# Weighted values as plain float32 products on TensorE, in place of float16 parts and DMA transposes

## The chip, the cores and the metric

The kernel runs on one core of one Trainium2 chip. The metric is the device time of one execution in microseconds (us); the time before is the median of three runs. Engines are named as in the profile: PE is the matrix engine, PEld its weight loads, DVE, ACT and POOL the vector, scalar and GpSimd engines, SP the queue that issues the DMAs.

## The reference

Attention over 2 batches of 8 heads, 576 positions and head size 64, and then two feed-forward blocks over the 1152 rows of 512 features:

```
q_rot, k_rot = rotate(q), rotate(k)                   # rotary embedding
scores = (q_rot @ k_rot.T) / 8
attn = exp(scores - max(scores)); attn /= sum(attn) + 1e-9
x = attn @ v                                          # heads side by side: 1152 x 512
x = ((x @ w_a) * (x @ w_b)) @ w_out                   # 512 -> 1536 -> 512
h = x @ w_in                                          # 512 -> 2048
out = (h * tanh(softplus(h))) @ w_out2                # 2048 -> 512
```

## The kernel before, in words

**Units.** The eight heads of a batch are handled as four pairs (p = 0 to 3 for batch 0, 4 to 7 for batch 1). A pair has nine units n: for each head four blocks of 128 query rows, and one unit "rest" that holds the last 64 rows of both heads. That makes 72 units, 36 in each batch. Each unit makes its scores on PE (tile `s`, two halves of 288 columns, a high and a low part of k each, so four matmuls), takes the row maximum (`m`, DVE), the exponential E (ACT), brings E to the layout with keys on the partitions, and multiplies it by V into tile `o` (`weighted`). V has a column of ones ahead of its 64 columns, so that column 0 of `o` is the sum. `finish` (L748) divides by it, and `transpose_x` turns the result into the columns of `x` that the feed-forward block reads.

**E transposed and multiplied.** Both operands are held as two float16 parts, high and low, and three partial products are added up. V is scaled by a power of two per pair (`v_max`, `v_scale`, `v_split`, L609 to L648; tile `vhl`) so that its parts fit float16. In batch 0 (`attend0`, L692) PE transposes E in float32 into PSUM (`tm`: four 128-column chunks of a unit; `tr`: the last chunk of two units together), ACT casts that to the high part and DVE subtracts for the low part (`ptm`, `ptr`); a unit has 15 float16 products. In batch 1 (`attend`, L725) ACT and DVE split E first (`pp`), and a DMA transpose on SP's queue writes the transposed parts (`pt`); a unit has 14 products there, the low parts against a second copy of V (`vh2`, L586) that `v_split` makes by DMA.

**Feed-forward.** Layer 1 and layer 2 of the first block (tile `l`, 1728 matmuls of 256 or 320 columns over both batches) and the second block (tiles `h` and `acc`) use float32 operands held as two reduced-precision parts in three passes. Each weight tile is unpacked by three DVE instructions (`xw`), cast by ACT and subtracted by DVE or POOL (`w`).

**Order.** The program is recorded as a list of operations with due times (`at(t)`) and costs (`Plan.cost`, L260), and `Plan.order` (L284) makes one fixed order per engine out of it: an operation is taken by due time among those that are ready by the planner's own clock. Operations marked `any` go to DVE or POOL and those marked `flex` to ACT or DVE, by the planner's costs. On the chip each engine works through its list strictly in that order. Layer 1 of batch 0 is put between the attention units of batch 1, since it needs only batch 0.

**PSUM.** `s` has two buffers of two banks, `o` one bank (a second one, `o2_ps`, in batch 1); in batch 0 `tm` has two and `tr` one, in batch 1 `l` has two.

Of the kernel before, what the change touches and what calls it, by code (L numbers as in the profile page):

```python
# [20 lines left out]
NP = H // 2  # L21
# [149 lines left out]
class Plan:  # L171
# [30 lines left out]
    def record(self, engine, method, args, kw):  # L202
# [26 lines left out]
        if key == "flex":  # L229

            scale = kw["scale"]
            forms = (
                ("act", "activation", args + (AF.Copy,), dict(scale=scale)),
                ("dve", "tensor_scalar_mul", args + (scale,), {}),
            )
            method, args, kw = forms[0][1:]
# [23 lines left out]
    def cost(self, key, method, out, args, kw, views):  # L260
# [146 lines left out]
VM = 4  # L407
# [10 lines left out]
VP = (10, 5, 8)  # L418
# [31 lines left out]
def kernel(ctx: ExitStack, tc: tile.TileContext, qk, v5, w1, w2, w34, tab, out):  # L450
# [34 lines left out]
    t_cm, t_ps = open_pool("t_ps", 1, space=PSUM)  # L485
    o2_ps = None
# [52 lines left out]
    ones = a_p.tile([8, 128], F32, tag="ones", name="ones")  # L539
# [7 lines left out]
    vhl = [(a_p if i < 2 else a0_p).tile([128, 5, 2, 130], F16, tag=f"vhl{i}", name=f"vhl{i}") for i in range(3)]  # L547

    vh2 = [a_p.tile([128, 4, 2, 66], F16, tag=f"vh2{i}", name=f"vh2{i}") for i in range(2)]

    vr = [a0_p.tile([128, 2, 130], F16, tag=f"vr{i}", name=f"vr{i}") for i in range(3)]
    vb = (0, 1, 2, 0, 1, 0, 1, 0)
# [18 lines left out]
    def load_v(p, pool_, tag, bufs):  # L571
        b, c = divmod(p, NP)
        t = pool_.tile([128, 512 if tag == "raw" else 5 * D], I64, tag=tag, name=f"v{p}", bufs=bufs)
        t = t.bitcast(F32)[:, 0 : 10 * D]
        sp.dma_start(t, v5[b, c].rearrange("p c h d -> p (c h d)"))
        return t
# [26 lines left out]

    v_mx = a_p.tile([128, B * NP], F32, tag="v_mx", name="v_mx")
    v_up = a_p.tile([128, B * NP], F32, tag="v_up", name="v_up")

    def v_max(p):  # L609
        if p < VM:  # L610

            of = vhl[min(p, len(vhl) - 1)].rearrange("p c h e -> p (c h) e")[:, :, 1 : D + 1]
            act.activation(of, v_t[p].rearrange("p (n d) -> p n d", d=D), AF.Abs, accum_out=v_mx[:, p : p + 1])
            return
        dve.tensor_reduce(v_mx[:, p : p + 1], v_t[p], axis=AX.X, op=ALU.max, apply_absolute_value=True)

    def v_scale(p0, p1):
        n, t = p1 - p0, o_ps.tile([128, 512], F32, tag="o", name=f"vs{p0}")
        m = a_p.tile([n, 1 + n], F32, tag=f"vm{p0}", name=f"vm{p0}")
        mx, up = v_mx[:, p0:p1], v_up[:, p0:p1]  # L620
        pe.matmul(t[0:n, 0:128], lhsT=mx, rhs=ident[:, 0:128], start=True, stop=True)
        dve.tensor_reduce(m[:, 0:1], t[0:n, 0:128], axis=AX.X, op=ALU.max)
        dve.tensor_scalar_mul(m[:, 1 : 1 + n], ident[0:n, 0:n], m[:, 0:1])
        pe.matmul(t[:, 128 : 128 + n], lhsT=ones[0:n, :], rhs=m[:, 1 : 1 + n], start=True, stop=True)
        dve.tensor_scalar(mx, t[:, 128 : 128 + n], 1e-30, 1e30, op0=ALU.max, op1=ALU.min)
        dve.tensor_scalar(mx.bitcast(U32), mx.bitcast(U32), 0x7F800000, None, op0=ALU.bitwise_and)
        dve.tensor_scalar_mul(mx, mx, 2.0**-14)
        dve.reciprocal(up, mx)

    def v_split(p):  # L630
        of = vhl[vb[p]].rearrange("p c h e -> p (c h) e")
        vt, up = v_t[p].rearrange("p (n d) -> p n d", d=D), v_up[:, p : p + 1]
        hi = of[:, :, 1 : D + 1]
        act.activation(hi, vt, AF.Copy, scale=up)
# [522 lines left out]
```

## Time and profile before

| what | value |
|---|---|
| time, median of 3 runs | 629.03 us (627.71 to 632.53) |
| time of the profiled execution | 626.95 us |
| its span, first to last instruction | 624.8 us |
| PE busy | 575.8 us (92%), 4384 matmuls |
| DVE busy | 493.1 us (79%) |
| ACT busy | 319.0 us (51%) |
| POOL busy | 127.4 us (20%) |
| granted clock, mean | 0.98 of full speed |

The span has four stretches, by what PE does: attention of batch 0 up to about 113 us; attention of batch 1 with layers 1 and 2 of batch 0 between its units, 113 to 295 us; the rest of the first block, 295 to 420 us; the second block from there. A busy PE is not a PE at its peak: a matmul's duration holds its way through the array, and the next one starts long before it ends. What PE can do is read from the distance of the starts in a dense stretch.

### The profile page before, as it was taken

Reading aid. Unit: us, or ns where it says so; the run is one execution under the profiler, and the core shown is the slowest. Engines: PE = TensorE matmul, PEld = TensorE weight load, DVE = VectorE, ACT = ScalarE, POOL = GpSimd, SP = SyncE. Lnnn points to the kernel's source line nnn. Section 1 sums busy time; section 2 is a strip of 40 time slices with the busy share of each in tenths; the row PEclk is TensorE's granted clock in tenths of the full one; section 3 lists DMA queues with packets and bytes.
Section 4 is the critical chain, followed back from the end, with each engine's and each line's share of the span. In section 5 each row is a group of like instructions: output and inputs, shape, how many; then the busy total and the mean of one; then the engine's idle time right before and its main releaser. Section 6 shows DMA issues by size and latency. Waiting matters only on the chain.

```text
span 624.8 us, 11406 instructions
## 1 busy us (share of the span) xinstructions
PE 575.8 (92%) x4384; PEld 526.8 (84%) x4384; DVE 493.1 (79%) x956; ACT 319.0 (51%) x629; POOL 127.4 (20%) x124
## 2 busy tenths in 40 slices
PE   6687888988898897999999999999999999999997
PEld 5576777987787786999999999997888899988985
DVE  6889989999899999999999999979999334332221
ACT  4978888674664754453344443246444444442320
POOL 5567683555315400120000001000000000000000
PEclk8898999999899898999999999999999999999999
DMA  8024212767569575879965557767897224220002
GB/s 300 6 72 163 87 41 69 213 144 204 144 155 250 136 176 123 203 184 242 375 210 201 171 202 231 292 203 252 277 301 264 67 69 152 77 75 1 0 1 84
DMA packets 78917, 100.27 MB, mean 160 GB/s; under 512 B 50832, under 2 KB 52496, under 8 KB 78864
## 3 DMA queue, kind: packets, MB, share of 16 engines
q1 hardware_dynamic: 78864, 99.55, 53.6%
q8 instruction: 34, 0.56, 0.4%
q14 instruction: 19, 0.16, 0.1%
HBM read 77.50 MB, written 10.75 MB: 141 GB/s over the span
## 4 chain that ended last, share of the span: by engine, by line
PE 65%; DVE 18%; ACT 8%; DMA 4%; POOL 3%; issue 2%; SPq 0%; POOLq 0%; DVEq 0%; ACTq 0%
PE l L389 28%; PE acc L389 16%; PE h L389 15%; DVE xw L389 5%; DVE m L389 3%; PE s L389 2%; PE o L389 2%; DMA pt<-pp 2%; ACT e L389 2%; POOL qkr L389 2%; DVE qk L389 2%; ACT qk L389 1%; DVE pp L389 1%; DVE w L389 1%; ACT ptm L389 1%
## 5 line engine op out<-in xcount | busy, mean ns | idle before, releaser
L389 PE MATMUL l<-x,w 128*128 128x256 f32 (+1 forms) x1152 | 169.2, 302 | 6.3 <-ACT w L389 2.3
L389 PEld LDWEIGHTS l<-x,w 128*128 128x128 f32 x1152 | 158.4, 192 | 8.6 <-DVE ab L389 2.8
L389 DVE SCALAR_TENSOR_TENSOR xw<-wr,xw 128x512 uint32<-128x512 uint32 x208 | 147.3, 722 | 1.0
L389 PE MATMUL h<-y,w 128*128 128x320 f32 (+1 forms) x576 | 105.0, 336 | 0.9 <-DVE g L389 0.9
L389 PE MATMUL acc<-w,g 128*128 128x512 f32 x432 | 105.6, 396 | 0.0
L389 PEld LDWEIGHTS h<-y,w 128*128 128x128 f32 x576 | 93.5, 188 | 10.4 <-DVE g L389 1.3
L389 ACT CAST w<-xw 128x512 fp32r<-128x512 f32 x97 | 59.8, 622 | 70.7 <-DVE xw L389 60.0
L389 PEld LDWEIGHTS acc<-w,g 128*128 128x128 f32 x432 | 80.6, 188 | 18.1
L389 PE MATMUL l<-ab,w 128*128 128x320 f32 (+1 forms) x576 | 80.2, 297 | 0.0
L389 PEld LDWEIGHTS l<-ab,w 128*128 128x128 f32 x576 | 77.2, 190 | 0.1
L389 DVE TENSOR_TENSOR w<-wc,w 128x512 fp32r<-128x512 f32 x39 | 26.7, 691 | 53.6 <-ACT w L389 52.3
L389 DVE TENSOR_TENSOR w<-xw,w 128x512 fp32r<-128x512 f32 x81 | 58.1, 722 | 5.6 <-ACT w L389 5.3
L389 PE MATMUL s<-qk 128*128 128x288 f32 x128 | 42.4, 345 | 14.6 <-ACT e L389 5.7
L389 DVE TENSOR_REDUCE m<-s 128x1 f32<-128x576 f32 x72 | 53.5, 748 | 2.7 <-PE s L389 2.4
L389 DVE TENSOR_SCALAR xw<-wr 128x512 uint32<-128x512 uint32 x104 | 51.7, 509 | 4.6 <-DMA wr<-in_w_dram 4.3
L389 ACT ACTIVATE h<-h 128x320 f32<-128x320 f32 (+1 forms) x48 | 22.8, 475 | 57.4 <-PE h L389 57.3
L389 DVE TENSOR_TENSOR g<-h,g 128x320 fp32r<-128x320 f32 (+1 forms) x48 | 26.6, 555 | 28.4 <-ACT g L389 28.3
L389 POOL TENSOR_TENSOR qkr<-qkr,cs 128x576 f32<-128x576 f32 x28 | 43.8, 1581 | 22.4 <-DMA qkr<-in_qk_dram 22.2
L389 PEld LDWEIGHTS s<-qk 128*128 128x128 f32 x128 | 25.8, 202 | 20.3 <-ACT e L389 9.0
L389 ACT ACTIVATE s<-s,m 128x576 f32<-128x576 f32 x36 | 25.7, 717 | 32.2 <-DVE m L389 31.7
L389 ACT CAST w<-wc 128x512 fp32r<-128x512 f32 x39 | 23.9, 617 | 35.6 <-PE acc L389 33.7
L389 POOL TENSOR_TENSOR w<-xw,w 128x512 fp32r<-128x512 f32 x16 | 20.5, 1280 | 96.8 <-ACT w L389 96.8
(93 smaller groups left out, 760.6 us busy)
## 6 DMA issues: line engine op xcount, KB each, us to landing
wr<-in_w_dram SPq DMA_DIRECT2D x104, 512.0 KB, 4.2
wc<-kc SPq DMA_DIRECT2D x39, 256.0 KB, 2.9
kc<-xw SPq DMA_DIRECT2D x32, 256.0 KB, 2.6
qkr<-in_qk_dram SPq DMA_DIRECT2D x14, 576.0 KB, 4.8
v<-in_v_dram SPq DMA_DIRECT2D x8, 320.0 KB, 6.4
out_dram<-o_sb SPq DMA_DIRECT2D x9, 256.0 KB, 2.1
pt<-pp SPq DMA_TRANSPOSE x36, 3.7
vh<-vhl SPq DMA_DIRECT2D x8, 66.0 KB, 2.3
```

Source lines behind the costliest of these rows:

```text
L389: getattr(engine, method)(*map(real, args), **{k: real(v) for k, v in kw.items()})
```

## The change

V is loaded as float32 straight into the tile `vt` (column 0 is set to ones once; three tiles in turn), by two DMAs per pair. `v_max`, `v_scale`, `v_split`, the scale `v_up`, the tiles `vhl`, `vr`, `vh2` and the tile `pp` are gone, and with them the 36 DMA transposes. Both batches go one way: E to SBUF in float32, PE transposes (`tm`, `tr`), one `flex` copy out of PSUM in float32 (`ptm`, `ptr`), and five plain float32 products per unit. In batch 0 the transposes have three PSUM buffers in common, in batch 1 one; the second `o` bank of batch 1 is gone. The planner's cost of a float32 matmul is set to four cycles per column. Due times, units and the feed-forward code stay.

```diff
@@ Plan.cost
-            return n * (2 if rhs.root.dtype == F32 else 1), n * rhs.a.shape[0] / 128
+            n *= 1 if rhs.root.dtype != F32 else 4 if method == "matmul" else 2
+            return n, n * rhs.a.shape[0] / 128
...
-    t_cm, t_ps = open_pool("t_ps", 1, space=PSUM)
-    o2_ps = None
+    t_cm, t_ps = open_pool("t_ps", 3, space=PSUM)
...
-    def load_v(p, pool_, tag, bufs):
+    def load_v(p):
         b, c = divmod(p, NP)
...
-        sp.dma_start(t, v5[b, c].rearrange("p c h d -> p (c h d)"))
-        return t
+        v = vt[p % 3]
+        sp.dma_start(v[:, 0:4, :, 1 : D + 1], v5[b, c, :, 0:4])
+        sp.dma_start(v[64:128, 4, :, 1 : D + 1], v5[b, c, 64:128, 4])
...
-    def v_max(p):
...
-    def v_split(p):
...
@@ weighted
-        ops = [(x, v, lo, w) for x, l, v in chunks for lo, w in ((0, D + 1), (D + 1, D)) if x is not None]
-        ops += [(x, v, 0, D + 1) for l, x, v in chunks if x is not None]
-        for i, (x, v, lo, w) in enumerate(ops):
+        for i, (x, v) in enumerate(chunks):
...
-            pe.matmul(oo, lhsT=x, rhs=rhs, start=(i == 0), stop=(i == len(ops) - 1))
+            pe.matmul(oo, lhsT=x, rhs=rhs, start=(i == 0), stop=(i == len(chunks) - 1))
...
-    def attend0(n):
+    def attend(n):
...
-            t = t_ps.tile([128, w], F32, tag=name, name=f"{name}{n}", bufs=bufs)
+            t = t_ps.tile([128, 512], F32, tag="t", name=f"{name}{n}")
             for i, b in enumerate(x):
                 pe.transpose(t[:, 128 * i : 128 * i + 128], b, ident[:, 0:128])
             at(t0_ + OFF["P"])
-            pt = a0_p.tile([128, 2, w], F16, tag=f"p{name}", name=f"p{name}{n}", bufs=6)
-            act.copy(pt[:, 0, :], t)
-            dve.tensor_tensor(pt[:, 1, :], t, pt[:, 0, :], op=ALU.subtract)
+            pt = pool_.tile([128, w], F32, tag=f"p{name}", name=f"p{name}{n}", bufs=bufs)
+            flex.copy(pt, t[:, 0:w], scale=1.0)
             return pt
...
-    def attend(n):
-
-        p = UNITS[n][0]
-        t0_ = t_unit(n)
-        e, m = scores(n)
-        act.activation(e, e, AF.Exp, bias=m)
-        at(t0_ + OFF["P"])
-        pp = a_p.tile([128, 2 * S], F16, tag="pp", name=f"pp{n}", bufs=3)
-        hi, lo = (pp[:, c : c + S].rearrange("p (a b) -> p a b", a=2) for c in (0, S))
-        act.copy(hi, e)
-        dve.tensor_tensor(lo, e, hi, op=ALU.subtract)
-        at(t0_ + OFF["T"])
-        pt = a_p.tile([128, 9, 128], F16, tag="pt", name=f"pt{n}", bufs=4)
-        sp.dma_start_transpose(out=pt, in_=pp)
...
-        dve.tensor_scalar(den, oo[:, :, 0], 1e-9, v_up[:, p : p + 1], op0=ALU.add, op1=ALU.mult)
+        dve.tensor_scalar_add(den, oo[:, :, 0], 1e-9)
...
             close_pool(t_cm)
             l_cm, l_ps = open_pool("l_ps", 2, space=PSUM)
-            o2_cm, o2_ps = open_pool("o2_ps", 1, space=PSUM)
+            t_cm, t_ps = open_pool("t2_ps", 1, space=PSUM)
...
-        if u == 3 and NP - 1 <= q < 2 * NP:
...
+        if u == V_AT and q < 2 * NP:
+            at(t_unit(n))
+            load_v(q)
```

The change moves instructions, since the planner's costs and the list change. First, PE's list in batch 1, at layer 1's third hidden block (tile `l`, then batch, block, half and operand in its name; `vhl` and `vh` are the float16 V, `pt` the transposed E). Before, one unit's products look like this, of which ten are against `vhl` and four against `vh`:

```order
L389 MATMUL s_2186<-qk_1402 128x288
L389 MATMUL s_2186<-kl_95,qk_1402 128x288
L389 LDWEIGHTS pt_2095
L389 MATMUL o_2134<-vhl_136,pt_2095 128x65
...
L389 MATMUL o_2134<-vhl_136,pt_2095 128x64
...
L389 MATMUL o_2134<-vh_1807,pt_2095 128x65
L389 MATMUL l_0_2_0_1_2214<-x_912,w_2072 128x256 x3
```

With the change, at the same block:

```order
L390 MATMUL tm_1711<-ident,e_1632 128x128 x4
L390 MATMUL l_0_2_1_0_1720<-x_724,w_1415 128x320 x3
L390 MATMUL l_0_2_1_0_1720<-x_1021,w_1415 128x320 x3
L390 MATMUL l_0_2_1_0_1720<-x_1229,w_1415 128x320 x2
L390 MATMUL tr_1735<-ident,e_1632 128x128
...
L390 MATMUL s_1744<-qk_1188 128x288
L390 MATMUL s_1744<-kl_95,qk_1188 128x288
...
L390 MATMUL o_1678<-vt_131,ptm_1671 128x65 x4
L390 MATMUL o_1678<-vt_131,ptr_1688 128x65
```

Fourteen products with float16 weights have become five with float32 operands, and transposes stand on PE between the `l` matmuls, ahead of the products that use them by a unit or more.

Second, DVE's list in batch 0, about the third and fourth pair of units (`ptm`, `ptr` the transposed E; `m` the row maximum; `v_mx`, `vm` the scaling of V). Before:

```order
L389 TENSOR_REDUCE vm_521<-vs_504 3x1
L389 TENSOR_TENSOR ptm_510<-tm_496,ptm_510 128x512
L389 TENSOR_REDUCE m_532<-s_515 128x1
L389 TENSOR_TENSOR ptm_530<-tm_508,ptm_530 128x512
L389 TENSOR_TENSOR ptr_538<-tr_525,ptr_538 128x256
L389 TENSOR_REDUCE m_556<-s_534 128x1
L389 TENSOR_TENSOR ptm_553<-tm_541,ptm_553 128x512
L389 TENSOR_SCALAR vm_521<-ident,vm_521 3x3
L389 TENSOR_REDUCE m_588<-s_558 128x1
```

With the change:

```order
L390 COPY ptm_410<-tm_396 128x512
L390 COPY ptr_418<-tr_404 128x256
L390 TENSOR_SCALAR den_r_425<-o_408 128x2
L390 RECIPROCAL den_r_425<-den_r_425 128x2
L390 TENSOR_REDUCE m_435<-s_422 128x1
L390 TENSOR_REDUCE m_461<-s_452 128x1
L390 COPY ptr_473<-tr_465 128x256
L390 TENSOR_SCALAR den_1_0_483<-o_442 128x2
```

The subtraction after each transpose and the scaling of V are gone from DVE; some of the copies out of PSUM stand there in their place (13 of 72 of `ptm` and 14 of 40 of `ptr` in the whole program; ACT has the others).

## Rows read from the trace of the kernel before

**Rows 1.** Busy time by stretch: PE, PEld, DVE, ACT, POOL; granted clock; DMA.

```profile
15.00:113.00 98.00, 79.25 (x929) 69.70 (x930) 89.59 (x184) 80.43 (x166) 60.94 (x61) 0.96 0.24 74
113.00:295.00 182.00, 161.89 (x1483) 152.14 (x1482) 173.42 (x344) 102.41 (x188) 56.29 (x37) 0.97 0.74 181
295.00:420.00 125.00, 125.00 (x933) 124.74 (x933) 118.51 (x237) 48.27 (x102) 2.08 (x4) 1.00 0.68 238
420.00:624.80 204.80, 199.84 (x1002) 172.01 (x1001) 102.05 (x177) 80.46 (x159) 0.00 (x0) 1.00 0.39 125
...
15.00:40.00 25.00, 16.96 (x153) 14.68 (x153) 22.02 (x41) 20.57 (x42) 13.35 (x12) 0.90 0.17 49
270.00:295.00 25.00, 24.65 (x253) 23.95 (x252) 23.92 (x50) 11.67 (x21) 5.16 (x4) 1.00 0.95 211
```

**Rows 2.** The chain of waits in order of time: start, length, what.

```profile
270.81 5.91 DMA pt<-pp
...
295.26 123.36 PE l L389 x924
```

**Rows 3.** Busy time by stretch, PE, matmuls that read or write tile l.

```profile
113.00:295.00 182.00, 122.64 (x786) 0.97 0.74 181
```

**Rows 4.** The same, tile s.

```profile
15.00:113.00 98.00, 30.88 (x160) 0.96 0.24 74
```

**Rows 5.** The same, tile o.

```profile
15.00:113.00 98.00, 26.03 (x540) 0.96 0.24 74
113.00:295.00 182.00, 24.08 (x504) 0.97 0.74 181
```

**Rows 6.** Timeline of PE in batch 0: start, length, what.

```profile
104.78 0.41 PE L389 MATMUL o<-vhl,ptm 128*128 128x65 f16 x8
...
105.24 0.63 PE L389 MATMUL tm<-ident,e 128*128 128x128 f32 x4
105.71 0.38 PE L389 MATMUL tr<-ident,e 128*128 128x128 f32 x2
```

**Rows 7.** Groups by form: times | busy us, mean ns | idle before.

```profile
L389 PE MATMUL tm<-ident,e 128*128 128x128 f32 x144 | 26.1, 294 | 4.7 <-ACT e L389 2.4 <-DVE ptm L389 2.0
L389 PE MATMUL tr<-ident,e 128*128 128x128 f32 x36 | 8.0, 278 | 0.1
L389 PE MATMUL vs<-ident,v_mx 128*1 128x128 f32 x10 | 2.1, 295 | 1.1 <-DVE xn L389 0.9 <-ACT ob L389 0.2
```

**Rows 8.** Timeline of PE and PEld at a float32 product of x.

```profile
290.01 0.30 PEld L389 LDWEIGHTS xt<-ident,xbd 128*128 128x128 f32 x2
...
290.12 0.33 PE L389 MATMUL xt<-ident,xbd 128*128 128x64 f32 x2
...
290.29 0.48 PE L389 MATMUL o<-vhl,pt 128*128 128x65 f16 x10
...
290.73 0.54 PE L389 MATMUL l<-ab,w 128*128 128x320 f32 x2
```

**Rows 9.** Instructions that touch xbd: shortest, median, longest in ns.

```profile
L389 PEld LDWEIGHTS xt<-ident,xbd x16: 188/191/192, 60.2 to 290.1; 128*128 128x128 f32 x16
L389 PE MATMUL xt<-ident,xbd x16: 221/248/275, 60.3 to 290.2; 128*128 128x64 f32 x16
```

**Rows 10.** Groups by form, DVE and ACT.

```profile
L389 DVE TENSOR_TENSOR pp<-s,pp 128x576 f16<-128x576 f32 x36 | 26.7, 748 | 0.2 <-ACT pp L389 0.2
L389 DVE TENSOR_TENSOR ptm<-tm,ptm 128x512 f16<-128x512 f32 x36 | 24.4, 681 | 1.9 <-ACT ptm L389 1.5
L389 ACT CAST ptm<-tm 128x512 f16<-128x512 f32 x36 | 20.9, 587 | 1.7 <-PE tm L389 1.6
```

**Rows 11.** Timeline of PE in the first stretch, with idle time before.

```profile
16.75 1.97 PE L389 MATMUL tm<-ident,e 128*128 128x128 f32 x8 [2.43 <-ACT e L389]
...
22.23 0.37 PE L389 MATMUL s<-qk,qz 128*128 128x288 f32 x1 [1.70 <-ACT e L389]
...
30.76 0.20 PE L389 MATMUL o<-vhl,ptm 128*128 128x65 f16 x1 [1.09 <-ACT vhl L389]
```

More of the change, by code (lines that the diff above doesn't have):

```diff
@@ L233, in record @@
                 ("act", "activation", args + (AF.Copy,), dict(scale=scale)),
-                ("dve", "tensor_scalar_mul", args + (scale,), {}),
+                ("dve", "tensor_copy" if scale == 1 else "tensor_scalar_mul", args + (() if scale == 1 else (scale,)), {}),
             )
@@ L405 @@
 HOLD = 40
-VM = 4
 KC = 320
@@ L546 @@
     xbd = [a_p.tile([128, 128], F32, tag=f"xbd{i}", name=f"xbd{i}") for i in range(2)]
[L547 to L552, printed above, removed]
+    vt = [a_p.tile([128, 5, 2, 66], F32, tag=f"vt{i}", name=f"vt{i}") for i in range(3)]
     istk = ident[:, 128:192]
@@ L602, in rope @@
                         act.copy(qz[p % 2][:, h, r], lo32(t[h][:, 512:576]))
-    v_mx = a_p.tile([128, B * NP], F32, tag="v_mx", name="v_mx")
-    v_up = a_p.tile([128, B * NP], F32, tag="v_up", name="v_up")
-    def v_max(p):
[L610 to L628, printed above, removed]
-    def v_split(p):
[L631 to L634, printed above, removed]
-        dve.scalar_tensor_tensor(of[:, :, D + 1 : 2 * D + 1], vt, up, hi, op0=ALU.mult, op1=ALU.subtract)
-        v = vhl[vb[p]]
-        if p < NP:
-            pool.tensor_copy(vr[vb[p]][64:128, :, 0 : 2 * D + 1], v[64:128, 4, :, 0 : 2 * D + 1])
-            return
-        v2 = vh2[vb[p]]
-        sp.dma_start(v2[0:64], v[64:128, 0:4, :, 0:66])
-        sp.dma_start(v2[64:128], v[0:64, 1:5, :, 0:66])
-        sp.dma_start(v[64:128, 4, :, 0 : 2 * D + 1], v[0:64, 0, :, 0 : 2 * D + 1])
     o_t, xn_t, den_t = {}, {}, {}
@@ L701, in attend0 @@
         t0_ = t_unit(n)
+        first = n < NU // 2
+        pool_ = a0_p if first else a_p
         j = 0 if rest else c % 2
@@ L704, in attend0, with turn @@
         if not j:
-            e_t[0] = a0_p.tile([128, 2, S], F32, tag="e", name=f"e{n}", bufs=3)
+            e_t[0] = pool_.tile([128, 2, S], F32, tag="e", name=f"e{n}", bufs=3 if first else 2)
         e = e_t[0]
         act.activation(e[:, j, :].rearrange("p (a b) -> p a b", a=2), s, AF.Exp, bias=m)
-        def parts(x, name, bufs):
+        def turn(x, name, bufs):
             w = 128 * len(x)
             at(t0_ + OFF["T"])
-            t = t_ps.tile([128, w], F32, tag=name, name=f"{name}{n}", bufs=bufs)
+            t = t_ps.tile([128, 512], F32, tag="t", name=f"{name}{n}")
             for i, b in enumerate(x):
@@ L914 @@
     load_qk(0, 0, ((QC, S),), tile=q0)
-    v_t[0] = load_v(0, a0_p, "v", 1)
+    load_v(0)
     sp.dma_start(ident, tab[:, 2 * S : 2 * S + 192])
-    pool.memset(ones, 1.0)
     for i in range(2):
@@ L922 @@
     for i in range(3):
-        pool.memset(vhl[i][:, :, :, 0:1], 1.0)
-        pool.memset(vr[i][0:64], 0.0)
+        pool.memset(vt[i][:, 0:4, :, 0:1], 1.0)
+        pool.memset(vt[i][0:64, 4], 0.0)
+        pool.memset(vt[i][64:128, 4, :, 0:1], 1.0)
     at(0)
@@ L933 @@
             rope(0, o, i, dve, slice(c0, c1))
-    at(VP[0])
-    v_max(0)
-    v_scale(0, 1)
-    v_split(0)
-    for p in range(1, NP):
-        at(VP[1])
-        v_t[p] = load_v(p, w_p, "raw", 3)
     def next_pair(p):
@@ L967 @@
             ab_cm, ab_p = open_pool("ab")
-        (attend0 if n < NU // 2 else attend)(n)
-        if n == V_AT:
-            at(t_unit(n) + VP[2])
-            for i in range(1, NP):
-                v_max(i)
-            v_scale(1, NP)
-            v_split(1)
-            v_split(2)
+        attend(n)
         for q, part, last, lag in XT:
```

34 lines of the change are left out of this document (8 added, 26 removed).

## The prediction

> **What bounds the kernel now.** I read the busy times by stretch first [rows 1]. Between 295 and 420 us PE is busy all the time, and the chain of waits shows one piece of 924 matmuls of tile `l` in 123.36 us [rows 2]: 0.1335 us from one to the next at 288 columns on average. There PE is the bound and runs without a hole. From 420 us on PE is busy too, and the change touches nothing. So what counts is 15 to 295 us. There DVE is the busiest: 89.59 of 98 us in batch 0, 173.42 of 182 us in batch 1, with PE at 79.25 and 161.89 [rows 1]. PE's busy time includes the way through the array, so I count what PE would need if everything stood as dense as it does elsewhere. `l` and `s` matmuls take 0.1335 us. Four transposes take from 105.24 to 105.71 us, 0.1175 us each [rows 6]. The 15 float16 products of a unit of batch 0 stand between 104.78 and 105.24 us, 0.46 us [rows 6]; the 14 of batch 1 between 290.29 and 290.73 us, 0.44 us [rows 8].
>
> - 15 to 113 us: 160 of `s` [rows 4] are 21.4 us, 144 + 36 transposes [rows 7] 21.2, 36 units of products 16.6; with the 19 first of `l` (2.5) and the transposes of x (4 x 0.1175 + 0.17, the float32 product below, 0.64 us a pair, three times) 64 us of 98. PE idles 34 us.
> - 113 to 295 us: 786 of `l` [rows 3] are 104.9 us, 160 of `s` 21.4 (as many as in batch 0), 36 units of products (504 [rows 5], 14 each) 15.8, five transposes of x 3.2: 145 us of 182. PE idles 37 us.
>
> So before, PE has 71 us of room ahead of 295 us, and DVE's list and the latencies fill them. The question is how much of that room the change uses up.
>
> **What it costs, on PE.** The nearest thing to the new product that the trace holds is the float32 product of x's last rows, `xt<-ident,xbd`, with 64 columns. There were eight of them and the profile shows 16 weight loads [rows 9]: a float32 product is two instructions, each with its own load of 128 float32 columns. The two loads take 0.30 us together [rows 8], one alone 0.191 us [rows 9], so the second starts 0.11 us after the first. A stream of such halves cannot go faster than its loads: 0.11 us each, 0.22 us a product, 1.1 us for the five of a unit. That is the upper of two bounds. The lower is the same pair seen from its neighbours: its first matmul starts at 290.12 us and the next tile's at 290.29 us [rows 8], 0.17 us a product, where the load of its first half went on under the work ahead of it. In a row of ten halves only the first has that cover, so I take 0.22. The 40 products of the units "rest" have 130 columns; two matmuls of 128 columns take 0.235 us as transposes do, so they get no price of their own.
> 360 products at 0.22 us are 79.2 us, against 36 x 0.46 + 36 x 0.44 = 32.4 us of float16 ones: +46.8 us. Batch 1 gets 180 transposes, as many as batch 0 has: 180 x 0.1175 = +21.2 us. The scaling of V leaves: one of the two kinds of its products is busy for 2.1 us [rows 7], so I give back nothing to 4 us and count 0. PE's work rises by 68 us.
> The Trainium skill, page "FP8 and Floating Point Precision", section "TensorE Precision Notes", says that a true float32 product is four passes through the array. By that alone a product of 65 columns at 2.4 GHz would be 65 x 4 / 2.4 = 108 ns, an estimate, and the sum would be some 40 us less. The trace has the two loads of a product 0.11 us apart beside that, so the measured price is kept.
>
> **What it saves.** DVE loses 36 subtractions of `pp`, 26.7 us, and 36 of `ptm`, 24.4 us [rows 10], besides those of `ptr` and the scaling of V. What comes back is a copy out of PSUM per group, 0.587 us by ACT's cast of the same size [rows 10]; in batch 0 it takes the place of that cast, in batch 1 that of the cast to `pp`. By the order most copies stand on ACT, which had 80.43 of 98 us in batch 0 and 102.41 of 182 in batch 1 [rows 1] and gets no more. Without those two groups alone DVE has 65 us left of 89.59, and 147 of 173.42. With 64 + 23 = 87 us in batch 0 and 145 + 23.8 + 21.2 = 190 us in batch 1, PE becomes the bound in both. The DMA transposes leave too. One of the last stands on the chain for 5.91 us from 270.81 us [rows 2], but PE idles only 0.35 us in all from 270 to 295 us [rows 1], as `l` matmuls fill that time; what it gives is in the holes below. The loads of V go out six units ahead of their use, some 16 us (98 us for 36 units), and cost nothing; only if SP's queue were that late would the first product of a pair wait.
>
> **Sum.** Without any hole PE would need 15 + 87 + 190 + 124 = 416 us up to where it now stands at 420 us. So the change can win 4 us at most if my price of a product holds, and every hole counts against it. Which holes stay? The first stretch, 15 to 40 us, waits for the exponentials of the first units: 2.43, 1.70 and, for the scaled V, 1.09 us [rows 11]; PE is busy there 16.96 of 25 us [rows 1], 8 us idle. The waits for V go, those for E stay; with the longer products I keep 8. For the other 250 us I take the rate of 270 to 295 us, where attention and `l` are mixed and DVE doesn't hold PE: 24.65 of 25 us busy [rows 1], 1.4% idle; doubled, because two of PE's waits are new (a copy out of PSUM stands between the transposes and the products, and in batch 1 the transposes have a single PSUM buffer), it is 3% or 8 us. So 416 + 16 = 432 us in place of 420: +12 us on the profiled execution's 626.95 (span 624.8, 2.15 around it), 639 us. The median of the runs shown is 2.1 us above that execution, and I put the median after at 640 us.
> The planner counts a product as 4 x 65 columns in one instruction, less than the 0.22 us of the rows. PE will therefore run late against the plan, and the other engines, being early, will seldom let it wait. That is why I don't keep more of the old idle time.
>
> **Rivals.**
> - *The halves overlap, and it gets faster.* If the second half of each product starts as in the pair by its neighbours, a product is 0.17 us, 360 are 61.2, and the sum is 18 us less: 622 us. For it: the 0.17 us are measured. Against: the load of the next product's first half has to wait for two loads ahead of it. It decides below 0.19 us a product, where the +12 turn into 0. Chance 0.16. If the loads cost nothing at all, the pair gives 0.33 - 0.275 = 0.055 us from one matmul's start to the next [rows 8, 9], 0.11 us a product, 39.6 us less than my 79.2: 600 us, chance 0.03. (That is near what the four passes of the Trainium skill's "FP8 and Floating Point Precision", "TensorE Precision Notes", would make of it.)
> - *PE is packed.* The holes shrink to 4 us or fewer because everything else is early: 627 to 630 us, no difference. For it: 295 to 420 us. Against: the first 25 us. Chance 0.13.
> - *The single buffer binds.* In batch 1 each group of transposes has to be copied out before the next one may start. If PE stands still for that, it is 0.587 us of copy and about 0.2 us around it per unit, 36 x 0.8 = 29 us in place of the 6 us that I allow there: 663 us. Against: in the order `l` matmuls stand between a group and the next. Chance 0.13.
> - The forecast, PE-bound with 8 to 28 us of holes: 630 to 652 us, chance 0.55.
>
> **Chances and range.** A difference of about 1%, 6.3 us, is what a measurement of this kernel can tell from none: 622.7 to 635.3 us is "same". Faster: 0.11 of the first rival and 0.03 of the loads at no cost, 0.14. Same: the rest of that rival, 0.05, the packed case, 0.13, and the lower fifth of the forecast, 0.10: 0.28. Slower: 0.58. The range of 8 in 10 leaves out the loads at no cost, the lower part of the first rival and the upper half of the third: 618 to 656 us.
>
> **What will show it.** Right: PE's list is two instructions for each product of `o`, with loads 0.11 us apart; five products of a unit span 1.0 to 1.2 us; PE is busy over 95% between 40 us and the last attention unit, with DVE at 60 to 80%; the unbroken run of `l` matmuls starts at 300 to 315 us in place of 295; everything behind it is shifted only. Wrong: products 0.17 us or closer, DVE still near 95%, idle time of PE put down to `ptm`, or a granted clock below the 0.96 and 0.97 of before [rows 1].

## The result, and the profile after

The changed kernel takes 635.4 us (median of 11 runs, 633.53 to 638.95) against 629.03 us (11 runs, 625.76 to 632.53). The ratio is 1.0101, with a 95% interval of 1.0076 to 1.0127: about 1% slower, at the border of what I had called "same". That is 6.4 us on the medians, where the forecast had 11. The profiled execution took 635.49 us, its span is 633.7 us, 8.9 us longer than that of before.

The page of the kernel after, its busy times and the chain that ended last by engine:

```profile
PE 616.1 (97%) x4216; PEld 581.9 (92%) x4216; DVE 446.8 (71%) x848; ACT 305.2 (48%) x606; POOL 117.5 (19%) x117
...
PE 90%; DVE 5%; ACT 1%; issue 1%; DMA 1%; SPq 0%; DVEq 0%; ACTq 0%
```

PE alone holds 90% of the chain now, 65% before. The stretches of the kernel after answer to [rows 1]: length, then busy time of PE, PEld, DVE, ACT and POOL with the number of instructions, granted clock, DMA share, GB/s. Batch 0 of the attention ends at about 104 us, batch 1 at 297.4 us; from 298.80 us on only `l` is left.

```profile
15.00:40.00 25.00, 23.48 (x182) 22.86 (x183) 17.54 (x29) 19.26 (x38) 15.83 (x16) 0.90 0.17 49
40.00:104.00 64.00, 62.91 (x540) 61.52 (x539) 49.08 (x94) 49.58 (x99) 41.93 (x42) 1.00 0.39 119
104.00:142.00 38.00, 36.29 (x283) 35.31 (x282) 35.74 (x56) 24.42 (x49) 25.14 (x16) 1.00 0.47 152
142.00:150.00 8.00, 7.45 (x34) 7.41 (x35) 4.76 (x10) 3.38 (x6) 0.00 (x0) 0.57 0.21 66
150.00:298.80 148.80, 146.26 (x1170) 144.34 (x1169) 111.85 (x234) 72.52 (x143) 25.27 (x17) 1.00 0.34 111
298.80:428.00 129.20, 129.20 (x968) 129.20 (x967) 115.27 (x230) 47.39 (x100) 1.81 (x4) 1.00 0.64 214
```

In the first 25 us PE is busy 23.48 us where it was 16.96 [rows 1]. In the long stretch of batch 1 it is busy 98% of the time, while DVE, which was busy 95% of batch 1 before, stands at 75%. The bound has gone over from DVE to PE; only from 104 to 142 us are both nearly full (36.29 and 35.74 of 38 us). The last `l` ends at 428.05 us in place of 418.62 us. The long piece of the chain of waits (start, length, what) answers to that of [rows 2]:

```profile
298.84 129.21 PE l L390 x966
```

It is longer by 42 matmuls of `l`, which stood between the units of batch 1 before.

One unit on PE in the kernel after, a timeline (start, length, what), answers to [rows 6]:

```profile
22.00 0.60 PE L390 MATMUL tm<-ident,e 128*128 128x128 f32 x4
22.43 1.00 PE L390 MATMUL o<-vt,ptm 128*128 128x65 f32 x8
23.27 0.39 PE L390 MATMUL o<-vt,ptr 128*128 128x65 f32 x2
23.47 0.38 PE L390 MATMUL s<-qk 128*128 128x288 f32 x1
```

The length in a row includes the way through the array; the next row's start tells what an instruction costs. Four transposes take from 22.00 to 22.43 us, 0.1075 us each (0.1175 in [rows 6]). The ten halves of the five products take from 22.43 to 23.47 us: 0.104 us a half, 0.208 us a product, 1.04 us a unit in place of 0.46.

What PE waits for in the kernel after, 15 to 298 us (us in total, times, longest):

```profile
PE tm L390 <- ACT e L390: 2.4, 1, 2.4
...
PE tr L390 <- ACT ptm L390: 2.0, 1, 2.0
...
PE l L390 <- DVE ab L390: 1.4, 2, 0.9
...
PE xt L390 <- DVE ptm L390: 0.8, 1, 0.8
```

The wait that a single buffer for the transposes would bring, `tm` or `tr` on a copy `ptm` or `ptr` unit after unit, occurred once in batch 1 (the 2.0 us of `tr`; waits too short to leave PE idle are not in this list). The copies themselves (shortest, median, longest in ns; first and last start), in answer to [rows 10]:

```profile
L390 ACT ACTIVATE ptm<-tm x59: 582/598/619, 19.8 to 291.1; 128x512 f32<-128x512 f32 x59
L390 DVE COPY ptm<-tm x13: 673/691/694, 20.4 to 262.1; 128x512 f32<-128x512 f32 x13
```

### The profile page after: what moved, and what is told of

Read it like the earlier page. It is cut to its first block, busy times and chain, and to the rows that moved or that the text cites. A ratio compares the mean times of both kernels' runs of the same rounds, so it can differ in the third digit from the quotient of the medians.

```text
span 633.7 us, 10846 instructions
## 1 busy us (share of the span) xinstructions
PE 616.1 (97%) x4216; PEld 581.9 (92%) x4216; DVE 446.8 (71%) x848; ACT 305.2 (48%) x606; POOL 117.5 (19%) x117
## 4 chain that ended last, share of the span: by engine, by line
PE 90%; DVE 5%; ACT 1%; issue 1%; DMA 1%; SPq 0%; DVEq 0%; ACTq 0%
PE l L390 35%; PE acc L390 16%; PE h L390 15%; PE o L390 12%; PE s L390 6%; PE tm L390 4%; DVE xw L390 2%; PE tr L390 1%; PE xt L390 1%; DMA qkr_k<-in_qk_dram 1%; DVE w L390 1%; DVE qk L390 1%; DVE m L390 1%; DVE kl L390 0%; ACT w L390 0%
## 5 line engine op out<-in xcount | busy, mean ns | idle before, releaser
L390 PE MATMUL l<-x,w 128*128 128x320 f32 (+1 forms) x1152 | 169.4, 301 | 1.4 <-DVE ab L390 1.4
L390 DVE SCALAR_TENSOR_TENSOR xw<-wr,xw 128x512 uint32<-128x512 uint32 x208 | 149.6, 732 | 1.4
L390 PE MATMUL h<-y,w 128*128 128x320 f32 (+1 forms) x576 | 104.8, 336 | 0.3 <-DVE g L390 0.3
L390 PE MATMUL o<-vt,ptm 128*128 128x65 f32 (+1 forms) x576 | 75.0, 271 | 1.9 <-DVE xbd L390 0.7
L390 PEld LDWEIGHTS o<-vt,ptm 128*128 128x128 f32 x576 | 71.8, 193 | 3.4 <-PE s L390 1.1
L390 DVE TENSOR_TENSOR w<-xw,w 128x512 fp32r<-128x512 f32 x86 | 61.6, 719 | 13.2 <-ACT w L390 13.2
L390 ACT ACTIVATE e<-s,m 128x576 f32<-128x576 f32 x72 | 52.9, 742 | 30.0 <-DVE m L390 26.9
L390 DVE TENSOR_SCALAR xw<-wr 128x512 uint32<-128x512 uint32 x104 | 50.2, 495 | 7.6 <-DMA wr<-in_w_dram 5.8
L390 ACT ACTIVATE h<-h 128x320 f32<-128x320 f32 (+1 forms) x48 | 22.8, 475 | 55.3 <-PE h L390 55.3
L390 PE MATMUL tm<-ident,e 128*128 128x128 f32 x288 | 45.4, 278 | 2.4 <-ACT e L390 2.4
```

The source lines that it names most:

```text
L390: getattr(engine, method)(*map(real, args), **{k: real(v) for k, v in kw.items()})
```

## The experiments

Times are medians; the ratio is to the kernel before on the same chip. "After" stands for the changed kernel. A difference to it sets medians from different chips side by side; the kernel before took 627.98 to 629.03 us on these chips, so about 1 us of such a difference need not be the edit's. The places below are starts read from PE's timelines of the profiled executions, one per kernel, in us: when the first product starts, the last product of batch 0, the last product of all, and the last `l`.

| kernel | first product | last of batch 0 | last product | last `l` |
|---|---|---|---|---|
| before | 30.8 | 109.4 | 292.8 | 418.3 |
| after | 22.4 | 103.4 | 297.4 | 427.7 |
| batch 0 alone in the new way | 23.8 | 108.0 | 286.5 | 415.9 |
| before, constant scale in batch 0 | 19.9 | 99.9 | 274.1 | 404.2 |
| before, constant scale for its first pair | 20.0 | 106.2 | 277.7 | 405.4 |
| before, first pair in the new way | 22.4 | 107.6 | 286.3 | 415.4 |
| after, scaling put back for the first pair | 27.2 | 104.8 | 302.0 | 432.4 |
| after, 3 of 5 products in batch 0 | 23.1 | 96.5 | 287.5 | 417.9 |
| after, 3 of 5 products in batch 1 | 22.5 | 103.5 | 276.3 | 406.7 |
| after, one subtraction per copy put back | 22.8 | 105.5 | 299.8 | 430.2 |
| after, PSUM buffers as before | 23.4 | 107.1 | 296.1 | 426.5 |

**One half of the change alone.** Batch 0 in the new way, batch 1 as in the kernel before, with its scaling pair by pair:

```diff
+SW = 4
...
-        attend(n)
+        (attend if p < SW else attend_old)(n)
```

> Batch 0 as in the changed kernel (float32 products, no scaling of V), batch 1 as in the kernel before (float16 parts, DMA transposes). Theory (the two stretches are worth what the traces show apart: batch 0's attention ends some 12 us earlier, 99.5 in place of 111.8 us, and batch 1 with its longer list on PE gives that back and 9 us more): about 12 us less than before, 615 to 619 us, with batch 1 again held by DVE. Rival (the 12 us are only borrowed, since DVE must still unpack the same weights and its list in batch 1 starts no earlier): 626 to 630 us, as before.

Measured: 620.48 us, ratio 0.9877 (0.9842 to 0.9912), between the two cases and nearer to the theory. So the two halves of the change pull apart: batch 0 in the new way wins 1.2%, and batch 1 in the new way costs 14.9 us on top of that (635.4 - 620.48). Where the 1.2% arises is less plain. By the table batch 0 ends 6.0 us earlier in the changed kernel (103.4 in place of 109.4 us; the expectation took 12), but only 1.4 us earlier in this one (108.0), though its units of batch 0 are the same. The planner orders the whole program anew for every edit, so differences of some microseconds between stretches can come from the order alone. The profiled execution of this kernel took 624.4 us, 3.9 us more than its median. The row of batch 1 in this kernel, columns as above:

```profile
108.00:286.50 178.50, 159.92 (x1452) 148.92 (x1451) 167.91 (x331) 99.40 (x184) 57.07 (x40) 0.96 0.79 176
```

DVE is the busiest again, 167.91 of 178.50 us, as before the change.

**Is PE the bound in batch 1?** Batch 1 of the changed kernel with three of its five products; two fifths of the keys are left out of the weighted sum there:

```diff
-            weighted(n if rest else n - 1 + i, chunks)
+            weighted(n if rest else n - 1 + i, chunks if first else chunks[0:2] + chunks[4:5])
```

> The changed kernel, with only three of the five products of each unit in batch 1; two fifths of the keys are left out there. 72 products, 144 halves, go. Theory (PE is the bound all through batch 1, so its work comes off the end one for one): 72 x 0.208 us = 15 us less than the changed kernel, 619 to 623 us. Rival (DVE's weights or the copies out of the single PSUM buffer hold batch 1): 0 to 5 us less, 630 to 635 us.

Measured: 614.74 us, ratio 0.9789 (0.9749 to 0.9828), 20.7 us below the changed kernel. The 72 products that are gone are 72 x 0.208 = 15 us; the trace of this run also has no stretch at the low clock like the one at 142 to 150 us above, which cost 3.4 us. The other 2 us were not followed. So a product's price is paid in full in batch 1. The whole of batch 1, and the run of `l` behind it in the chain of waits (start, length, what), show that only attention became shorter; the run of `l` has the same 129.21 us as in the changed kernel and starts 21.05 us earlier:

```profile
103.50:276.30 172.80, 170.40 (x1337) 167.12 (x1336) 149.75 (x288) 100.35 (x199) 58.77 (x40) 1.00 0.40 130
...
277.79 129.21 PE l L390 x966
```

**What sets the price of a product?** In batch 1, 128 more float32 products of one column, each after a product with the same weights:

```diff
             pe.matmul(oo, lhsT=x, rhs=rhs, start=(i == 0), stop=(i == len(chunks) - 1))
+            if p >= NP and not rest and i < len(chunks) - 1:
+                pe.matmul(oo[:, 0:1], lhsT=x, rhs=rhs[:, 0:1], start=False, stop=False)
```

> The changed kernel, with 128 more float32 products in batch 1 (four in each of the 32 units that are not a rest), each of one column only, added into the sum of the weights, which is wrong by it. Theory (two weight loads of 0.104 us set the price of a product, whatever its columns): 128 x 0.208 = 27 us more than the changed kernel, 658 to 666 us. Rival (the columns that stream set it: 65 columns in four passes are 108 ns a product and the rest is overhead that adds up elsewhere): a product of one column costs next to nothing, 635 to 640 us.

Measured: 660.32 us, ratio 1.0507 (1.0453 to 1.0561), 24.9 us above the changed kernel: 0.195 us for a product that has 1 column in place of 65. Its timeline on PE shows the same from row to row:

```profile
239.87 0.78 PE L390 MATMUL o<-vt,ptm 128*128 128x65 f32 x6
240.49 0.28 PE L390 MATMUL tr<-ident,e 128*128 128x128 f32 x1
240.60 1.18 PE L390 MATMUL o<-vt,ptm 128*128 128x1 f32 x10
241.64 0.41 PE L390 MATMUL o<-vt,ptr 128*128 128x65 f32 x2
```

(The name of the form is that of a row's first instruction; the ten halves are mixed, every other pair has one column.) Ten halves from 240.60 to 241.64 us, 0.104 us each, exactly as with 65 columns throughout. From 1 to 65 columns the columns cost nothing; the two loads of the weights are left as the price. The small products of V's scaling in the kernel before bear this out, and show where it ends:

```profile
102.35 0.09 PEld L389 LDWEIGHTS vs<-ident,v_mx 128*1 128x1 f32 x2 [0.47 <-ACT ob L389]
103.69 0.29 PEld L389 LDWEIGHTS vs<-vm,ones 1*128 1x128 f32 x2
...
102.35 0.38 PE L389 MATMUL vs<-ident,v_mx 128*1 128x128 f32 x2 [0.23 <-ACT ob L389]
```

One load of one column takes 0.082 us and one of 128 columns 0.182 us (medians), so the second load of a pair starts 0.01 us after the first with one column of weights and 0.11 us after it with 128. But the first of these products sends 128 columns through the array, and its two matmuls (0.27 us for one) start 0.11 us apart although their loads are short. So 65 columns go unnoticed under the loads; at 128 the columns alone would cost as much.

**Does DVE matter in batch 0?** One subtraction per transposed copy put back on DVE in batch 0, 31.9 us of work whose result nobody reads (24.3 us behind `ptm`, 7.6 us behind `ptr`):

```diff
             flex.copy(pt, t[:, 0:w], scale=1.0)
+            if first:
+                lo = a0_p.tile([128, 512], F16, tag="lo", name=f"lo{name}{n}", bufs=2)[:, 0:w]
+                dve.tensor_tensor(lo, t[:, 0:w], pt, op=ALU.subtract)
```

> The changed kernel, with one subtraction put back on DVE behind each copy out of PSUM in batch 0, of the size that the kernel before had there (into a tile that nobody reads): 36 x 0.68 + 20 x 0.39 = 32 us of DVE, which has 57 of 78 us now between 22 and 100 us. Theory (batch 0 became shorter because DVE lost this work): DVE would need 89 us in place of 78, so 10 to 15 us more than the changed kernel, 645 to 650 us. Rival (it became shorter because the scaling of V and its waits left the start, and because the transposes have three buffers in common): 0 to 4 us more.

Measured: 638.96 us, ratio 1.0167 (1.0131 to 1.0204), only 3.6 us more than the changed kernel. The work is there (36 of 128x512, shortest, median and longest in ns), and DVE still has room in 22 to 100 us, 68.15 of 78 us (second line; the third is the changed kernel):

```profile
L390 DVE TENSOR_TENSOR lotm<-tm,ptm x36: 664/680/694, 21.5 to 103.2; 128x512 f16<-128x512 f32 x36
...
22.00:100.00 78.00, 75.57 (x646) 73.94 (x646) 68.15 (x137) 64.64 (x128) 45.22 (x46) 1.00 0.28 85
22.00:100.00 78.00, 77.43 (x663) 75.77 (x660) 57.17 (x111) 62.87 (x124) 49.56 (x49) 1.00 0.37 113
```

DVE has only 11 us more to do there, as the planner gave most of the copies to ACT and put less work on the weights into this stretch. Batch 0 ends 2.1 us later by the table. So this much work finds room on DVE; whether a list as full as before's would hold batch 0 is not shown.

**Is PE the bound in batch 0?** The cut to three products of five, this time in batch 0 (two fifths of the keys are left out there):

```diff
+            weighted(n if rest else n - 1 + i, chunks[0:2] + chunks[4:5] if first else chunks)
```

> The changed kernel, with only three of the five products of each unit in batch 0; two fifths of the keys are left out there. Theory (PE is the bound in batch 0 too, from 22 us on): 72 x 0.208 = 15 us of PE go, and 12 to 16 us come off, 619 to 624 us. Rival (the pace of batch 0 is set by DVE, ACT or POOL with their latencies, at 71.5, 71.5 and 61 of 93 us, and PE only just keeps up): 0 to 6 us less, 629 to 635 us.

Measured: 626.66 us (10 runs), ratio 0.9967 (0.9948 to 0.9986), 8.7 us below the changed kernel, between the two cases. Of the 15 us of products 6.9 us came back by the end of batch 0 (103.4 to 96.5 us); with the time as a whole, more than half. PE then is no longer full in 22 to 95 us:

```profile
22.00:95.00 73.00, 66.79 (x537) 62.89 (x536) 62.35 (x115) 59.93 (x121) 47.14 (x47) 1.00 0.36 112
```

PE 66.79, DVE 62.35, ACT 59.93 of 73 us: batch 0 sits close to a balance. Take 15 us off PE, and the waits on the other engines keep half of them.

**Where did the first pair's 8 us come from?** First the kernel before with a constant 2^14 as the scale of V in batch 0. The float16 parts of V are still made; what is gone is the search for the largest value, its two small products on PE and five small steps on DVE (that scale fits the data of this case, not any data):

```diff
-    v_max(0)
-    v_scale(0, 1)
+    pool.memset(v_up[:, 0:NP], 2.0**14)
     v_split(0)
...
-            for i in range(1, NP):
-                v_max(i)
-            v_scale(1, NP)
             v_split(1)
```

> The kernel before, with the maximum and the scale of V in batch 0 replaced by a constant 2**14 that is written at the start (the split into float16 parts stays; batch 1 stays). By the traces the changed kernel ends the first pair of heads 8 us earlier (42.0 in place of 49.9 us) and takes no less for each later pair. Theory (the chain of the scaling at the start held the first pair): 5 to 8 us less than before, 620 to 623 us. Rival (DVE's subtractions in the first pair, or the PSUM buffers): 0 to 2 us less, 626 to 629 us.

Measured: 611.86 us, ratio 0.9737 (0.9705 to 0.9769): 16.8 us won, more than either case expected, and the fastest kernel of this study. Its first 25 us, in answer to the fifth line of [rows 1]:

```profile
15.00:40.00 25.00, 22.93 (x229) 20.51 (x230) 23.07 (x43) 22.03 (x45) 16.64 (x17) 0.86 0.25 78
```

PE is busy 22.93 us in place of 16.96 and gets through 229 instructions in place of 153. Why a few small steps cost so much is seen on DVE's timeline of the kernel before:

```profile
22.38 0.19 DVE L389 TENSOR_SCALAR vm<-ident,vm 1x1 f32<-1x1 f32 x1
...
24.75 0.15 DVE L389 TENSOR_SCALAR v_mx<-vs 128x1 f32<-128x1 f32 x1
24.81 0.75 DVE L389 TENSOR_REDUCE m<-s 128x1 f32<-128x576 f32 x1
25.48 0.14 DVE L389 TENSOR_SCALAR v_mx<-v_mx 128x1 uint32<-128x1 uint32 x1
25.65 1.40 DVE L389 SCALAR_TENSOR_TENSOR qk<-qkr,qk 64x576 fp32r<-64x576 f32 x1
27.08 0.15 DVE L389 TENSOR_SCALAR v_mx<-v_mx 128x1 f32<-128x1 f32 x1
28.26 0.69 DVE L389 TENSOR_TENSOR ptm<-tm,ptm 128x512 f16<-128x512 f32 x1 [1.03 <-ACT ptm L389]
28.87 0.15 DVE L389 RECIPROCAL v_up<-v_mx 128x1 f32<-128x1 f32 x1
```

Five steps of 0.14 to 0.19 us, 0.8 us of work, take from 22.38 to 29.02 us, because DVE works in order and has long instructions between them. Only then can V be scaled, and the first product starts at 30.76 us [rows 11]. The last wait, 1.09 us, was the only part of that which the profile put down to V. The step ahead of these five, a reduction of 0.27 us, had started at 16.51 us already.

Then the same for the first pair alone:

```diff
-    v_max(0)
-    v_scale(0, 1)
+    pool.memset(v_up[:, 0:1], 2.0**14)
     v_split(0)
```

> The kernel before with a constant scale for V of the first pair of batch 0 alone; the other three pairs of batch 0 are scaled as before. Theory: what the constant scale for four pairs won (16.8 us) is the wait of the first products for the first scaled V and what follows from it, so nearly all of it comes with the first pair alone: 611 to 615 us, first product at 20 us, last product of batch 0 some 9 us earlier than in the kernel before. Rival: only the 9 us by which the first pair ends earlier come with it, and the other 7 to 8 us are the work of the other three scalings on DVE and ACT: 618 to 621 us.

Measured: 615.38 us, ratio 0.9804 (0.9782 to 0.9826): 12.8 us won, between the two cases and nearer to the theory. By the table only 3.2 us of it are there at the end of batch 0, where the theory had 9 (with the constant scale for all four pairs it is 9.5 us of the 16.8). The other part comes in batch 1, whose own work is unchanged: from the last product of batch 0 to the last of all it takes 171.5 us in place of 183.4, of which 2 us are 15 matmuls of `l` that went behind it. The stretch in the kernel before and in this kernel:

```profile
109.40:292.80 183.40, 163.15 (x1495) 153.25 (x1492) 174.61 (x345) 103.59 (x192) 57.48 (x39) 0.97 0.74 179
106.20:277.70 171.50, 156.33 (x1472) 145.75 (x1469) 165.21 (x331) 101.16 (x189) 62.33 (x44) 1.00 0.79 189
```

and in the kernel with the constant scale for all of batch 0:

```profile
99.90:274.10 174.20, 157.97 (x1466) 149.15 (x1462) 168.21 (x339) 101.74 (x191) 60.25 (x42) 0.97 0.80 185
```

DVE, the bound there, has 9.4 and 6.4 us less to do than in the kernel before (174.61 us). In the first of the two half of that is six subtractions for the weights (`w`) that no longer stand on DVE in this stretch, five of them on POOL: the planner shares out the work anew when the start has changed. The granted clock is no common cause: 0.97 in the kernel before and in the second of these, 1.00 in the first, where it may have a part. Which change of the order did the rest stays open. So 12.8 and 16.8 us are what the two kernels won, not the price of the wait alone.

Then the scaling put back into the changed kernel for its first pair, without the float16 parts:

```diff
-    load_v(0)
+    sp.dma_start(v0, v5[0, 0].rearrange("p c h d -> p (c h d)"))
...
+    act.activation(of[:, 0:8], raw[:, 0:8], AF.Abs, accum_out=v_mx)
...
+    dve.reciprocal(v_up, v_mx)
+    act.activation(of[:, 0:8], raw[:, 0:8], AF.Copy, scale=v_up)
```

> The changed kernel with the scaling put back for the first pair alone: V is loaded into a buffer of its own, its largest value is found on ACT, passed through the two small products on PE and the steps on DVE, and ACT writes V times the scale in float32; no second float16 part, all products as in the changed kernel. Theory: the 8 us of holes that were kept in the forecast and did not stay are the wait for this chain; with it back the first product moves from 22 to about 30 us and the time rises by 6 to 10 us, to 641 to 645 us. Rival: the changed kernel's first pair is earlier because DVE has fewer subtractions; then putting the scaling back costs 0 to 2 us.

Measured: 640.18 us, ratio 1.0193 (1.0171 to 1.0215): 4.8 us more than the changed kernel, on the theory's side but short of its 6 to 10. (The chain is not the old one step for step: ACT accumulates the magnitudes of four of the five chunks of V, where DVE took the largest value of all.) The first product moves from 22.4 to 27.2 us, and not to 30. At the end of batch 0 only 1.4 us of that are left by the table (104.8 in place of 103.4), and 4.6 us at the last product, so the delay at the start did not simply run through to the end. In the first stretch PE idles 3.0 us with the chain in place of 1.5, not 8:

```profile
15.00:40.00 25.00, 22.01 (x165) 20.90 (x166) 18.10 (x37) 18.59 (x36) 13.59 (x13) 0.91 0.16 49
```

The row of the first product shows the wait that is back; again only its last 0.33 us are put down to V:

```profile
27.25 1.08 PE L390 MATMUL o<-vt,ptm 128*128 128x65 f32 x8 [0.33 <-ACT vt L390]
```

**The first pair alone in the new way**, the rest as in the kernel before:

```diff
+            if p == 0:
+                pt = pt.rearrange("p a b -> p (a b)").bitcast(F32)
+                act.copy(pt, t)
+                return pt
...
+        if p == 0:
+            ops, chunks = [(x, v, 0, D + 1) for x, v in chunks], []
```

> The kernel before with the first pair of batch 0 alone in the way of the change: no scale and no parts of V for it, plain float32 products; all other pairs as before. Theory: PE has idle time only in the first pair (16.96 of 25 us busy there), so the 9 units of longer products, 9 x 0.58 = 5 us of PE's time, fit into it, and the wait for the scaled V is gone: the last product of the first pair 7 to 9 us earlier than in the kernel before, 612 to 621 us, below both kernels and below the one with the whole of batch 0 in the new way (620.5). Rival: the 5 us are paid in full, because the pair is bound by PE once V is there: 5 us more than the constant scale of the first pair alone gives.

Measured: 624.5 us (9 runs), ratio 0.9948 (0.9931 to 0.9965): 3.6 us won, 9.1 us less won than with the constant scale of that pair. That is above the theory's range and more than the rival's 5 us. The first product does start at 22.4 us, and PE's idle time took up the longer products, but DVE stood idle for part of it. Stretch 31 to 42 us of this kernel:

```profile
31.00:42.00 11.00, 10.18 (x80) 8.94 (x79) 5.28 (x14) 8.88 (x19) 7.67 (x9) 1.00 0.01 3
```

and of the kernel with the constant scale of the first pair:

```profile
31.00:42.00 11.00, 10.25 (x89) 8.97 (x87) 10.32 (x21) 10.26 (x20) 9.00 (x8) 1.00 0.18 55
```

PE is as busy in both, 10.2 us. But in the first DVE has 5.28 us of work in place of 10.32. In part that is work it no longer has: ten subtractions, 5.6 us, fall into this stretch in the second kernel and none in the first. In part it waits, and what it waits for stands behind the long row of float32 products on PE: the copies `ob` of their sums, and the `s` of the second pair (waits of DVE from 30 to 60 us: total, times, longest):

```profile
DVE den L389 <- ACT ob L389: 3.4, 4, 2.8
DVE m L389 <- PE s L389: 1.5, 1, 1.5
```

So PE's idle time was not quite free room: PE had to feed DVE, which is busy for 46.7 of the 50 us from 50 to 100 us. But that can explain little of the 9.1 us. By the table batch 0 ends 1.4 us later than with the constant scale (107.6 and 106.2 us). The greater part, 7.2 us, comes in batch 1, whose own work is the same in both kernels (178.70 us in place of 171.50, with 171.36 us of DVE in place of 165.21):

```profile
107.60:286.30 178.70, 159.66 (x1470) 149.55 (x1468) 171.36 (x341) 101.51 (x191) 52.31 (x37) 0.97 0.80 183
```

It is the same effect of the order as above, and its cause stays open.

**Buffers in PSUM.** The changed kernel with two buffers for `tm` and one for `tr` in batch 0, as before, in place of three for both:

```diff
-            t = t_ps.tile([128, 512], F32, tag="t", name=f"{name}{n}")
+            if first:
+                t = t_ps.tile([128, w], F32, tag=name, name=f"{name}{n}", bufs=2 if name == "tm" else 1)
```

> The changed kernel, with batch 0's PSUM buffers for the transposes shared out as before: two for the four chunks of a unit, one for the last chunks, in place of three in common. Theory (the scaling of V is what held the first pair): 0 to 2 us more than the changed kernel, 635 to 638 us. Rival (the common buffers are what let the first pair through): 5 to 8 us more, 640 to 644 us.

Measured: 633.66 us, ratio 1.0092 (1.0061 to 1.0124), no slower than the changed kernel. So the buffers explain nothing of the time as a whole. Within batch 0 they can't be ruled out: it ends 3.7 us later with them (107.1 in place of 103.4 us), more than with the scaling (1.4) or the subtractions (2.1) put back, and batch 1 makes up for it, in a trace that has no low clock after 22 us. With batch 0 alone in the new way it ends at 108.0 us with the same units and buffers, so the order may have done this too.

**A failed middle way.** Two of the four pairs of batch 1 in the old way, to take 20 us off PE where it binds (with room in SBUF, fewer buffers for it, and V's parts made late):

```diff
+SW = 6
...
+        (attend if p < SW else attend_old)(n)
```

> Batch 0 and the first two pairs of batch 1 in the new way, the last two pairs of batch 1 in the old one (with two buffers for the float16 E and three for its transposed parts, one fewer each, and V's split made only where the old way begins, for space). In the run with batch 0 alone in the new way, batch 1 had DVE busy 168 of 180 us and PE 162. Theory (DVE holds the old way and PE the new one, so a mixture that loads both is shorter than either): two pairs take 18 x 0.75 = 13.5 us and V's preparation, 4 us, from DVE and bring PE 18 x 1.24 = 22 us that it has idle: 6 to 10 us less than with batch 0 alone, 610 to 615 us. Rival (the fewer buffers and the late split of V, or PE's holes that don't close, cost as much): 618 to 624 us.

Measured: 650.83 us, ratio 1.0357 (1.0328 to 1.0387), worse than either case. Around the switch, at 142 to 205 us, PE is idle for 17 of 63 us and the granted clock is at its low level for half of that time:

```profile
142.00:160.00 18.00, 15.04 (x113) 14.50 (x114) 10.57 (x22) 12.71 (x24) 1.47 (x2) 0.88 0.00 1
160.00:205.00 45.00, 31.06 (x217) 26.73 (x216) 30.97 (x70) 18.48 (x30) 1.41 (x2) 0.67 0.56 135
```

Neither PE nor DVE is full there, so it looks as if the hand-over, not the mix, was measured; of the wanted balance the run says nothing.

## Why the prediction came out as it did

The forecast was right in direction and near in size: 12 us on the profiled execution against 8.9 us of span, 640 us against 635.4 on the medians, where the difference was 6.4 us in place of 11. That it came so near is in part luck, as the errors in its terms went both ways. By its own steps:

- **PE becomes the bound in both batches.** Right for batch 1, shown by the cut to three products (the price is paid in full) and by DVE's 111.85 of 148.8 us. In batch 0 only half right: there the same cut gave back 8.7 of 15 us, and 6.9 by the end of batch 0.
- **A product at 0.22 us.** Right in kind, two loads a product and nothing for the 65 columns, and 6% too high: 0.208 us, so 360 of them were 4.3 us too dear. The rivals with overlapping halves and with free loads are refuted by the row of ten halves, and by the one-column products. By the four passes that the Trainium skill names ("FP8 and Floating Point Precision", section "TensorE Precision Notes") I had estimated 108 ns a product; the trace has twice that, and a product of one column costs as much. What agrees is the Trainium skill's page "TensorE: Matmul & The Clock Gate", section "LDWEIGHTS (loading the stationary operand)", by which a load takes its number of columns divided by 1.2, in ns: 107 ns for 128, where the trace has 104 ns from half to half. For the float16 weights of the kernel before the trace does not agree: 15 products with as many columns of weights each take 0.46 us [rows 6], 31 ns a product.
- **A transpose at 0.1175 us.** 0.1075 us in the kernel after; for all 360 the sum was 3.6 us too high.
- **The holes.** 16 us were kept, 8 of them in the first stretch. There PE idles only 25 - 23.48 = 1.5 us now: this step failed. I had said that the waits for E stay and are the most of it. Of those in [rows 11] the one of 2.43 us stayed, and it ends at 15.5 us now; the others went. I had read 1.09 us off [rows 11], the last piece of the wait for the scaled V, and had priced the scaling by its own work, 0 to 4 us, counted as 0. The kernel before starts its products 10.8 us earlier without that chain, and with it the changed kernel starts them 4.8 us later. But the chain explains the 8 us only in the kernel before: put back into the changed kernel it brings PE's idle time there from 1.5 to 3.0 us and the time up by 4.8 us. What else closed the holes there, the longer products or DVE's shorter list, was not taken apart. So the mis-sized term is the 8 us of holes in the first stretch, which measured 1.5 us.
- **The sum.** With the measured prices PE needs 401 - 4.3 - 3.6 = 393 us from 15 us on, where the forecast had 401. It took 413 us (15 to 428), 20 us more. Of these, 3.4 us are the stretch at 142 to 150 us with a granted clock of 0.57 (8 x 0.43), which I had not foreseen there, and up to 2.5 us the first stretch with 0.90 (25 x 0.10), which the sum priced at the full clock though [rows 1] had 0.90 too. 14 us remain, where 16 were forecast; but only 7.4 us are idle in the rows above (1.5 in the first stretch, 5.9 from 40 to 298.8 us), and the other 6.6 lie inside what is shown as busy. They may be short waits that the way through the array covers; that was not followed. So the total of the holes came out near by luck, with two errors in it: too much in the first stretch, too little elsewhere. 432 - 7.9 + 3.4 + 2.5 - 2 = 428 us.
- **The single buffer.** Refuted by the waits (one, of 2.0 us, in batch 1). The run with other buffers changed batch 0 alone and says nothing on it.
- **What DVE saves.** Worth little once PE binds, as forecast: 31.9 us put back in batch 0 cost 3.6 us, with the planner's help, which moved other work off DVE.
- **The signs named beforehand.** Units of 1.04 us (1.0 to 1.2), PE at 97.7% and DVE at 78% from 40 to 298.8 us (over 95%, 60 to 80%) came true. The unbroken run of `l` starts at 298.84 us, just ahead of the 300 to 315 us named, as the sum was 4 us too high.

So the change does two things. It takes a chain of small steps out of the way of the first products, and it puts more work on PE: 36 units of products in each batch at 1.04 us in place of 0.46 and 0.44, and 180 transposes. In batch 0 PE had room, and the first wins by a little (620.48 us, batch 0 alone). In batch 1 it had not. With the constant scale in place of the scaling, the old way comes to 611.86 us. The rest of the change then costs 635.4 - 611.86 = 23.5 us. These two don't quite add up as parts, since the old way with a constant scale still makes its float16 parts, and since 9.2 us of what the constant scale won arise in batch 1 (174.20 us in place of 183.40), whose own work it leaves as it was.

## What to carry to other kernels

Price a small scalar chain by the place it has in the queue, not by its work: five steps of 0.15 us took 6.6 us on an engine that works in order, and the profile put down only the last microsecond of it to its cause. Before moving work onto an engine with idle time, ask what that idle time feeds: DVE waited where PE took up the longer products. And try a change of two parts one part at a time; here one half was worth 7.5 us and the other cost 14.9. But where a planner orders the program anew for each edit, look at where a difference arises before giving it to the edit: of the 9.1 us between two kernels that differ in their first pair, 7.2 arose in a stretch with the same instructions.

## What the runs showed that I had not expected

A float32 product costs the same with 1 and with 65 columns, 0.104 us a half. The granted clock fell to its low level from 142.8 to 149.7 us in the kernel after, with PE busy for 36.29 of the 38 us ahead of it, and for 34 us of the 63 us from 142 to 205 us in the middle way that failed, where PE was idle more. And a kernel that starts its first products 10.8 us earlier, with the same instructions in batch 1, went through batch 1 in 11.9 us less, with 9.4 us less work on DVE; what in the order led to that was not found.
